# Attention with pooled keys, top-k rows and an MLP: high and low values side by side in one product, the scaling of the rows moved to ScalarE, one turned tile in the last batch

## The chip, the cores and the metric

One core of one Trainium2 chip. The time is device microseconds of one execution: 983.64 us before, the median of 3 runs (982.88 to 988.36). The names of the engines in the rows are PE (TensorE, with PEld for its weight loads), DVE (VectorE), ACT (ScalarE), POOL (GpSimd) and SP (SyncE, which issues the DMAs).

## The reference

```python
def _attn_ref(q, kv, w_sr):          # q: 4 x 12288 x 128, kv: 4 x 384 x 32 x 128
    kv_pool = kv.reshape(B, H // r, r, W // r, r, C).mean(axis=(2, 4))   # r = 4
    kv_flat = kv_pool.reshape(B, -1, C) @ w_sr                           # 768 keys of 128
    k = v = kv_flat
    s = scale * (q @ k.transpose(0, 2, 1))
    s = s - s.max(-1, keepdims=True)
    a = np.exp(s)
    a /= a.sum(-1, keepdims=True) + 1e-09
    return a @ v

def _moe_ref(x, w_gate, w1, w2, capacity):   # capacity = 128 rows per batch
    scores = np.einsum('bsd,d->bs', x, w_gate)
    out = x.copy()
    for b in range(B):
        top_idx = np.argpartition(-scores[b], capacity)[:capacity]
        xe = x[b, top_idx]
        ye = np.maximum(xe @ w1, 0.0) @ w2
        g = 1.0 / (1.0 + np.exp(-scores[b, top_idx]))
        out[b, top_idx] = x[b, top_idx] + g[:, None] * ye
    return out
```

The result is float32. Nearly all of the work is the attention: 49,152 queries against 768 keys of their batch.

## The kernel before, in words

**Tiling.** The four batches are cut into 192 blocks of 256 queries, 48 blocks per batch. A block has two halves (j = 0 and 1) of 128 queries, and the 768 keys make KT = 6 tiles of 128. The scores of a block, two halves of 768 columns, fill three PSUM banks; there are two such buffers (`s_buf`, s in the rows), used by turns. The remaining two banks are `o_two`, one for the output of each half. It exists once.

**Exactness by splitting.** Scores are made of three products (`S`): high query by low key (kl), low query (ql) by rounded key (kb), and high query by high key (kh). The exponentials are split into a float16 high part `ah` and a bfloat16 low part `al`, the values into a high and a low float16 part `vx[0]` and `vx[1]`. Each value tile has VC = 130 columns: 128 values, a column of ones (whose product is the sum of the weights), and the gate's score of the key. The low part has 0 in the column of ones.

**A block's way.** `S` writes the scores on PE. `s_max` takes the negated maximum of each half on DVE (m in the rows). `exp` makes the exponentials on ACT in three parts, part 2 (512 columns, the last bank) first, then part 1 and part 0 (am in the rows). The weights must then be turned so that keys lie on the partitions. Most tiles are turned by a DMA transpose (`turn`, rows at<-hl): ACT copies the high part (`to_high`), POOL or DVE subtracts to get the low part (`to_low`), and one transpose for each follows. The last `turned(n)` key tiles of a block are turned on PE instead (`turn_pe`, rows s<-cst,am): 1 in even blocks and 2 in odd blocks of batches 0 to 2, none in batch 3. They go from PSUM straight into `at` (rows at<-s). Where fewer than two are turned, part 1 (`own`, 256 columns) goes through its own copies (rows hl<-s). `AV` multiplies turned weights by values: per half, 6 x 2 products of `ah` by high and low values, then 6 of `al` by high values, all 130 columns wide, summed in one bank of `o_two`.

**The end of a block.** `sums` and `recip` make the reciprocal rz of the sums on DVE. `finish` multiplies the gate's column (rows sc<-o_two,rz) and the 128 columns of both halves (rows x<-o_two,rz) by rz, both on DVE. Four blocks share one tile x, which SP then stores.

**Order.** A helper (L54 in every row) chains the instructions of each engine in the order in which the program issues them, so each compute engine works in written order. Iteration i of the main loop writes s_max(i), AV of block i-4, the exponentials of block i, PE's turned tiles, scores of block i+1 in four parts, the end of block i-4, and the copies of block i. The turned tiles stand on PE behind the first of the four score parts. In front of every second block's exponentials ACT splits the queries of two blocks (`split_q`, rows qh<-q_raw). Three side tasks run in slots between: the next batch's keys (pooling on POOL, projection on PE, copies on ACT, rows kv_proj, kh, kb, vx), the top-k search of the batch before (rows junk, up, th, cnt), and its MLP. SP's order is not written out; the scheduler that builds the program places the DMAs.

Of the kernel before, what the change touches and what calls it, by code (L numbers as in the profile page):

```python
# [6 lines left out]
F32 = mybir.dt.float32  # L7
F32R = mybir.dt.float32r
F16 = mybir.dt.float16
# [4 lines left out]
AF = mybir.ActivationFunctionType  # L14
# [5 lines left out]
P = 128  # L20
# [48 lines left out]
def attention_topk_mlp(ctx, tc, a, outs, capacity):  # L69
# [34 lines left out]

    o_two = ps_o.tile([P, QT, 512], F32, name="o_two")
    o_all = o_two[:, :, 0:VC]
    banks = [o_two[:, j] for j in range(QT)]
    room = {"used": False}

# [33 lines left out]
    def new_keys(b):  # L143
        kvset[b] = {
            "kh": keys.tile([P, M], F32R, name="kh"),
            "kl": keys.tile([P, M], BF16, name="kl"),
            "kb": keys.tile([P, M], BF16, name="kb"),
            "raw": keys.tile([P, KT, 2, P], F32, name="kv_proj"),
            "vw": keys.tile([P, KT], F32, name="vw"),
            "mx": keys.tile([P, 4], F32, name="mx"),  # L150
            "vx": keys.tile([P, 2, KT, VC], F16, name="vx"),
            "sg": keys.tile([P, 4], F32, name="sg"),
        }

# [232 lines left out]
        st[n] = {"m": m}  # L387

    def turned(n):
        return 0 if blocks[n][0] == B - 1 else 1 + n % 2  # L390

    def own(n):
        return OWN if turned(n) < 2 else 0
# [59 lines left out]
    def turn(n, h):  # L453
        nc.sync.dma_start_transpose(out=st[n]["at"][:, h, 0:QT * KT - turned(n)], in_=st[n]["hl"][:, h, 0:main(n) + own(n)])

    def AV(n, j, dest=None):
        vx = kvset[blocks[n][0]]["vx"]
        assert kvset[blocks[n][0]].get("ready")
        ah, al = (st[n]["at"][:, h, j * KT:(j + 1) * KT].bitcast(t) for h, t in enumerate((F16, BF16)))
        if j == 0:  # L460
            st[n]["o"] = o_all if dest is None else dest
        o = st[n]["o"][:, j]
        tiles = list(range(KT))
        if j and own(n):
            tiles = tiles[2:KT - turned(n)] + tiles[0:2] + tiles[KT - turned(n):]
        mm = [(ah, h, kt) for kt in range(KT) for h in range(2)] + [(al, 0, kt) for kt in range(KT)]
        for i, (w, h, kt) in enumerate(mm):
            pe.matmul(o, w[:, kt], vx[:, h, tiles[kt]], start=(i == 0), stop=(i == len(mm) - 1))
# [11 lines left out]
    def finish(n):  # L480
        b, blk = blocks[n]
        o, rz = st[n]["o"], st[n]["rz"]
        if blk % GROUP == 0:
            xt_[b] = ob.tile([P, GROUP * QT, C], F32, name="x")
        x = xt_[b]
        if b not in scores:
            scores[b] = tk.tile([P, NCOL], F32, name="sc")
        if n < nb - 2:
            dve.tensor_tensor(out=scores[b][:, blk * QT:(blk + 1) * QT], in0=o[:, :, C + 1], in1=rz, op=ALU.mult)
        dve.tensor_tensor(out=x[:, (blk % GROUP) * QT:(blk % GROUP + 1) * QT], in0=o[:, :, 0:C], in1=rz.rearrange("p (j o) -> p j o", o=1).broadcast_to([P, QT, C]), op=ALU.mult)  # L490
        if blk % GROUP == GROUP - 1:
            ch, h = divmod(blk // GROUP, BPC // GROUP)
            nc.sync.dma_start(out=outs[b].rearrange("(h p j) d -> h p j d", p=P, j=JPC)[ch, :, h * GROUP * QT:(h + 1) * GROUP * QT], in_=x)
        del st[n]

    def topk(b):
# [167 lines left out]
    nc.sync.dma_start(out=w1, in_=a["w1"])  # L664
    nc.sync.dma_start(out=w2, in_=a["w2"].rearrange("(t f) d -> f t d", f=P))

    select, prep, vals, ended = [], [], [], []

    def start(tasks, gen):
        tasks.append([gen, next(gen)])  # L670
# [7 lines left out]
    def at_point(point):  # L678
        advance(vals, point)
        advance(prep, point)  # L680
        advance(select, point)
# [4 lines left out]
    for i in range(nb):  # L686
# [66 lines left out]
        else:  # L753
# [3 lines left out]
                dve.tensor_tensor(out=l, in0=x, in1=h, op=ALU.subtract)  # L757
            turn(i, 0)
            turn(i, 1)
        at_point("d")  # L760
        if old and blocks[m][1] == NBLK - 1:
            start(select, topk(blocks[m][0]))
# [120 lines left out]
```

## Time and profile before

| | |
|---|---|
| median of 3 runs | 983.64 us (982.88 to 988.36) |
| the profiled execution | 982.0 us, its span 980.2 us |
| granted TensorE clock, mean of the span | 0.973 |
| PE busy | 901.0 us (92%), 9995 products |
| DVE busy | 741.5 us (76%) |
| ACT busy | 749.0 us (76%) |
| POOL busy | 719.9 us (73%) |
| chain that ended last | PE 61%, DMA 13%, DVE 12%, ACT 6%, issue 5% |
| DMA | 216.02 MB, 384 transposes, 4.4 us from issue to landing in the median |

All rows are of the one profiled execution. The span is the time from its first to its last instruction. Busy is time in which an engine worked on at least one instruction; products overlap in PE's pipeline, so one product's duration is longer than the time until the next begins. Batches 0, 1 and 2 end near 250, 485 and 725 us, the last block's products near 936, and behind it stand the last batch's top-k and MLP.

### The profile page before, as it was taken

The page shows a single profiled execution, that of the slowest core. Times are in us where ns is not written, and L with a number is a line of the kernel's source. Part 1 is how long each engine was busy: PE and PEld are TensorE (multiplying, and loading weights), DVE is VectorE, ACT ScalarE, POOL GpSimd, SP SyncE. Part 2 cuts the span into 40 slices and gives each one's busy share as a digit, 9 for nine tenths or more (in the row PEclk, how much of TensorE's full clock was granted, in tenths as well). Part 3 has the DMA queues.
Part 4 walks back from the last instruction along what each step waited for, and adds up shares of the span by engine and source line. Part 5 has one row for each costly group of instructions (what it writes and reads, how often), then busy time and mean ns, then how long its engine had stood idle before and what let it go on. Part 6 is the DMA issues. An engine that isn't in the chain of part 4 may idle for free.

```text
span 980.2 us, 25939 instructions
## 1 busy us (share of the span) xinstructions
PE 901.0 (92%) x9995; PEld 719.2 (73%) x9995; DVE 741.5 (76%) x2000; ACT 749.0 (76%) x1241; POOL 719.9 (73%) x487
## 2 busy tenths in 40 slices
PE   4799899999999999999899999999899999999844
PEld 4577777777778778787677777787687777777743
DVE  5766677667788788788778877888868878778775
ACT  2588688888988787888788887888798878978600
POOL 2588788887788888888688886888678767767500
PEclk9999999999999999999999999999999999999976
DMA  9899999999999999999979999999899999999910
GB/s 357 215 236 223 233 231 240 256 230 244 226 227 231 241 233 243 243 233 233 219 169 232 240 234 230 225 216 201 191 190 227 235 240 236 235 244 221 220 28 6
DMA packets 568540, 216.02 MB, mean 220 GB/s; under 512 B 549216, under 2 KB 550368, under 8 KB 567648
## 3 DMA queue, kind: packets, MB, share of 16 engines
q1 hardware_dynamic: 568160, 213.84, 104.4%
q8 instruction: 78, 1.28, 0.5%
q0 software_dynamic: 256, 0.52, 0.2%
q14 instruction: 46, 0.38, 0.1%
HBM read 52.04 MB, written 25.43 MB: 79 GB/s over the span
## 4 chain that ended last, share of the span: by engine, by line
PE 61%; DMA 13%; DVE 12%; ACT 6%; issue 5%; POOL 2%; SPq 0%; POOLq 0%; DVEq 0%; ACTq 0%
PE s L54 34%; PE o_two L54 27%; DMA at<-hl 11%; DVE m L54 6%; ACT am L54 3%; DMA kv_raw<-in_kv 2%; ACT hl L54 1%; DVE junk L54 1%; POOL ql L54 1%; DVE sg L54 1%; ACT s L54 1%; DVE idx L54 1%; DVE hl L54 1%; POOL kv_sum L54 0%; DVE mg L54 0%
## 5 line engine op out<-in xcount | busy, mean ns | idle before, releaser
L54 POOL TENSOR_TENSOR hl<-am,hl 128x1280 bf16<-128x1280 f32 (+1 forms) x191 | 483.3, 2530 | 186.4 <-ACT hl L54 153.4
L54 PEld LDWEIGHTS <-at 128*128 128x128 f16 (+1 forms) x6912 | 401.4, 97 | 75.2 <-issue 48.9
L54 PE MATMUL o_two<-vx,at 128*128 128x130 f16 x6804 | 436.2, 220 | 19.1 <-DMA at<-hl 17.0
L54 DVE TENSOR_REDUCE m<-s 128x2 f32<-128x1536 f32 x192 | 337.2, 1757 | 114.0 <-PE s L54 113.5
L54 ACT ACTIVATE am<-s,m 128x512 f32<-128x512 f32 (+2 forms) x456 | 332.0, 744 | 105.0 <-DVE m L54 96.7
L54 PE MATMUL s<-kh,qh 128*128 128x512 f32 (+1 forms) x768 | 364.1, 476 | 0.0
L54 PE MATMUL s<-kl,qh 128*128 128x512 bf16 (+1 forms) x768 | 257.1, 335 | 3.0 <-DVE hl L54 1.7
L54 PE MATMUL s<-kb,ql 128*128 128x512 bf16 (+1 forms) x768 | 252.2, 328 | 1.1 <-POOL ql L54 0.9
L54 ACT CAST hl<-am 128x1152 f16<-128x1152 f32 (+1 forms) x192 | 236.1, 1230 | 2.3
L54 PEld LDWEIGHTS s<-kh,qh 128*128 128x128 f32 x768 | 147.3, 192 | 49.8 <-issue 1.4
L54 POOL TENSOR_TENSOR ql<-q_raw,qh 128x512 bf16<-128x512 f32 x96 | 122.7, 1278 | 6.2 <-ACT qh L54 6.2
L54 PEld LDWEIGHTS <-qh 128*128 128x128 bf16 x768 | 78.1, 102 | 32.7 <-issue 16.0
L54 PEld LDWEIGHTS <-ql 128*128 128x128 bf16 x768 | 76.2, 99 | 9.2 <-issue 3.6
L54 DVE TENSOR_TENSOR x<-o_two,rz 128x256 f32<-128x256 f32 x189 | 78.3, 414 | 0.0
L54 DVE TENSOR_TENSOR at<-s,at 128x128 bf16<-128x128 f32 (+1 forms) x144 | 51.2, 356 | 31.2 <-ACT at L54 29.2
L54 ACT CAST at<-s 128x128 f16<-128x128 f32 (+1 forms) x144 | 45.9, 319 | 35.0 <-PE s L54 34.7
L54 PE MATMUL s<-cst,am 128*128 128x128 f32 x216 | 53.6, 303 | 13.7 <-ACT am L54 13.1
L54 DVE TENSOR_SCALAR rz<-o_two,sg 128x2 f32<-128x2 f32 x189 | 40.9, 216 | 31.7 <-PE o_two L54 31.3
L54 PEld LDWEIGHTS s<-cst,am 128*128 128x128 f32 x216 | 26.2, 141 | 48.6 <-ACT am L54 45.2
L54 ACT CAST qh<-q_raw 128x512 fp32r<-128x512 f32 x96 | 59.2, 617 | 1.1 <-DMA q_raw<-in_q 1.1
L54 ACT ACTIVATE s<-s,m 128x256 f32<-128x256 f32 x120 | 53.8, 448 | 3.9
L54 POOL TENSOR_TENSOR kv_sum<-kv_raw 128x256 f32<-128x256 f32 x72 | 53.1, 737 | 0.0
(171 smaller groups left out, 622.9 us busy)
## 6 DMA issues: line engine op xcount, KB each, us to landing
out<-x SPq DMA_DIRECT2D x48, 512.0 KB, 3.7
q_raw<-in_q SPq DMA_DIRECT2D x46, 512.0 KB, 5.5
kv_raw<-in_kv SPq DMA_DIRECT2D x36, 512.0 KB, 5.1
kv_raw<-in_kv SPq DMA_DIRECT2D x6, 1024.0 KB, 7.3
at<-hl SPq DMA_TRANSPOSE x384, 4.4
w<-in_w SPq DMA_DIRECT2D x2, 512.0 KB, 9.1
q_raw<-in_q SPq DMA_DIRECT2D x1, 768.0 KB, 8.3
cst<-in_cst SPq DMA_DIRECT2D x1, 320.0 KB, 9.7
```

What stands on the lines that cost most here:

```text
L54: r = f(*args, **kwargs)
```

## The change

The tile vx keeps the high and the low half of each key tile side by side, and in the main loop one product of 260 columns multiplies `ah` by both; the output of a half then has 260 columns in its bank. The six products of `al` by the high half stay as they were and are added to the first 130 columns. `finish` no longer reads the finished sum from PSUM: DVE adds the two groups of 130 columns into a new SBUF tile t (a reduction over pairs that lie 130 columns apart), takes the gate's column from t, and ACT scales the 128 columns of each half by rz, one ACTIVATE per half. These two are issued at the end of the iteration, behind the copies of block i, and the store follows them. The last four blocks keep the old form. In batch 3 one key tile per block is turned on PE instead of none.

```diff
+    o_pair = o_two[:, :, 0:2 * VC].rearrange("p j (h c) -> p j c h", h=2)
...
-            "vx": keys.tile([P, 2, KT, VC], F16, name="vx"),
+            "vx": keys.tile([P, KT, 2, VC], F16, name="vx").rearrange("p t h c -> p h t c"),
...
     def turned(n):
-        return 0 if blocks[n][0] == B - 1 else 1 + n % 2
+        return 1 if blocks[n][0] == B - 1 else 1 + n % 2
...
+        if dest is None:
+            o = o_two[:, j, 0:2 * VC]
+            for kt in range(KT):
+                pe.matmul(o, ah[:, kt], vx[:, :, tiles[kt]].rearrange("p h c -> p (h c)"), start=(kt == 0), stop=False)
+            for kt in range(KT):
+                pe.matmul(o[:, 0:VC], al[:, kt], vx[:, 0, tiles[kt]], start=False, stop=(kt == KT - 1))
+            return
...
+        if not ended:
+            t = ob.tile([P, QT, VC], F32, name="t")
+            dve.tensor_reduce(out=t, in_=o_pair, axis=AX.X, op=ALU.add)
+            dve.scalar_tensor_tensor(out=gate, in0=t[:, :, C + 1], scalar=1.0, in1=rz, op0=ALU.mult, op1=ALU.mult)
+
+            def scaled():
+                for j in range(QT):
+                    act.activation(rows[:, j], t[:, j, 0:C], AF.Copy, scale=rz[:, j:j + 1])
+                store()
+
+            late.append(scaled)
+        else:
+            if n < nb - 2:
+                dve.tensor_tensor(out=gate, in0=o[:, :, C + 1], in1=rz, op=ALU.mult)
+            dve.tensor_tensor(out=rows, in0=o[:, :, 0:C], in1=rz.rearrange("p (j o) -> p j o", o=1).broadcast_to([P, QT, C]), op=ALU.mult)
+            store()
...
+        while late:
+            late.pop(0)()
         at_point("d")
```

How it moves the instructions is shown at three places. The first is ACT around the end of an odd block of batch 1 (s_111) and the start of the even one (s_110): hl is the copy of the high weights, qh the split of the queries, am and s the exponentials. Before:

```order
L54 ACTIVATE am<-s_111,m 128x768
L54 CAST hl<-am 128x1280
L54 CAST qh<-q_raw 128x512
L54 ACTIVATE am<-s_110,m 128x512
L54 ACTIVATE s_110<-s_110,m 128x256
```

And now:

```order
L54 ACTIVATE am<-s_111,m 128x768
L54 CAST hl<-am 128x1280
L54 ACTIVATE x<-t,rz 128x128 x2
L54 CAST qh<-q_raw 128x512
L54 ACTIVATE am<-s_110,m 128x512
L54 ACTIVATE s_110<-s_110,m 128x256
```

Two instructions now stand between hl and qh, and so ahead of the even block's first exponential; in even blocks they stand between hl and the odd block's first exponential.

The second place is DVE in a block of batch 3, from the reciprocal's input to the next maximum; up, th and junk belong to the top-k search. Before:

```order
L54 TENSOR_SCALAR junk,cnt<-key,th 128x96
L54 TENSOR_SCALAR rz<-o_two,sg 128x2
L54 RECIPROCAL rz<-rz 128x2
L54 TENSOR_TENSOR sc<-o_two,rz 128x2
L54 TENSOR_TENSOR x<-o_two,rz 128x256
L54 TENSOR_REDUCE m<-s_111 128x2
```

And now:

```order
L54 TENSOR_SCALAR junk,cnt<-key,th 128x96
L54 TENSOR_SCALAR rz<-o_two,sg 128x2
L54 RECIPROCAL rz<-rz 128x2
L54 TENSOR_REDUCE t<-o_two 128x260
L54 SCALAR_TENSOR_TENSOR sc<-t,rz 128x2
L54 TENSOR_TENSOR at<-s_110,at 128x128
L54 TENSOR_REDUCE m<-s_111 128x2
```

The reduction t takes the place of x as the last reader of o_two, sc now reads t, and the low part of the turned tile stands ahead of the next maximum.

The third place is SP in batch 3: transposes (at), stores (out) and loads of queries (q_raw). Before:

```order
L493 DMA out<-x 128x1024
L454 DMA_TRANSPOSE at<-hl 128x12x128 x2
L139 DMA q_raw<-in_q 128x1024 x2
L454 DMA_TRANSPOSE at<-hl 128x12x128 x6
L493 DMA out<-x 128x1024
```

And now:

```order
L501 DMA out<-x 128x1024
L455 DMA_TRANSPOSE at<-hl 128x11x128
L140 DMA q_raw<-in_q 128x1024
L455 DMA_TRANSPOSE at<-hl 128x11x128 x2
L140 DMA q_raw<-in_q 128x1024
L455 DMA_TRANSPOSE at<-hl 128x11x128 x5
L501 DMA out<-x 128x1024
```

The store goes behind the first transpose of a block instead of ahead of it, and the two loads of queries no longer follow each other. Over the whole program two loads of queries stand back to back 18 times before and 4 times now, with two transposes between them 4 times before and 18 times now. Two loads of raw keys stand back to back 5 times before and 10 times now.

## Rows read from the trace of the kernel before

**Rows 1.** Page, part 1: engine, busy us (share of the span), instructions.
```profile
PE 901.0 (92%) x9995; PEld 719.2 (73%) x9995; DVE 741.5 (76%) x2000; ACT 749.0 (76%) x1241; POOL 719.9 (73%) x487
```

**Rows 2.** Waits, 60 to 725 us: who waited for whom: us, times, longest.
```profile
PEld s L54 <- ACT am L54: 39.8, 96, 3.3
...
PE o_two L54 <- DMA at<-hl: 13.1, 15, 2.5
```

**Rows 3.** Timeline of ACT, batch 1: start us, duration us, instruction [idle before].
```profile
308.20 1.26 ACT L54 CAST hl<-am 128x1280 f16<-128x1280 f32 x1
309.36 0.61 ACT L54 CAST qh<-q_raw 128x512 fp32r<-128x512 f32 x1
310.21 0.69 ACT L54 ACTIVATE am<-s,m 128x512 f32<-128x512 f32 x1 [0.24 <-DVE up L54]
...
312.53 1.17 ACT L54 CAST hl<-am 128x1152 f16<-128x1152 f32 x1
```

**Rows 4.** Timeline of PE in the same even block.
```profile
308.17 1.20 PE L54 MATMUL o_two<-vx,at 128*128 128x130 f16 x18
...
309.24 1.19 PE L54 MATMUL o_two<-vx,at 128*128 128x130 f16 x18
...
310.95 0.33 PE L54 MATMUL s<-cst,am 128*128 128x128 f32 x1
311.12 0.27 PE L54 MATMUL s<-kl,qh 128*128 128x256 bf16 x1
311.23 0.27 PE L54 MATMUL s<-kb,ql 128*128 128x256 bf16 x1
```

**Rows 5.** Timeline of DVE, the odd block's end, the even block and the next maximum.
```profile
307.05 0.16 DVE L54 TENSOR_TENSOR sc<-o_two,rz 128x2 f32<-128x2 f32 x1
307.12 0.42 DVE L54 TENSOR_TENSOR x<-o_two,rz 128x256 f32<-128x256 f32 x1
...
308.36 1.76 DVE L54 TENSOR_REDUCE m<-s 128x2 f32<-128x1536 f32 x1 [0.49 <-PE s L54]
...
312.69 1.76 DVE L54 TENSOR_REDUCE m<-s 128x2 f32<-128x1536 f32 x1 [0.78 <-PE s L54]
```

**Rows 6.** Timeline of ACT, an even block near the start of batch 1.
```profile
255.61 0.41 ACT L54 CAST vx<-kv_proj 128x256 f16<-128x256 f32 x1
255.92 0.61 ACT L54 CAST qh<-q_raw 128x512 fp32r<-128x512 f32 x1
256.44 0.68 ACT L54 ACTIVATE am<-s,m 128x512 f32<-128x512 f32 x1
```

**Rows 7.** Timeline of DVE, the maxima of that even block and the next.
```profile
254.08 1.76 DVE L54 TENSOR_REDUCE m<-s 128x2 f32<-128x1536 f32 x1 [0.55 <-PE s L54]
...
258.92 1.76 DVE L54 TENSOR_REDUCE m<-s 128x2 f32<-128x1536 f32 x1 [0.79 <-PE s L54]
```

**Rows 8.** Groups by line and shape: count | busy us, mean ns | idle before.
```profile
L54 ACT ACTIVATE kv_proj<-kv_proj,sg 128x256 f32<-128x256 f32 x9 | 4.6, 512 | 0.0
...
L54 DVE TENSOR_REDUCE mg<-s 128x2 f32<-128x256 f32 x4 | 1.6, 412 | 0.0
```

**Rows 9.** Timeline of SP in batch 3, DMA issues.
```profile
772.83 1.00 SPq L139 DMA_DIRECT2D q_raw<-in_q  x2
773.93 10.22 SPq L454 DMA_TRANSPOSE at<-hl  x4
```

**Rows 10.** Timeline of PE behind those loads.
```profile
783.69 0.52 PE L54 MATMUL o_two<-vx,at 128*128 128x130 f16 x6 [1.90 <-DMA at<-hl]
...
784.08 2.09 PE L54 MATMUL o_two<-vx,at 128*128 128x130 f16 x18
```

**Rows 11.** Timeline of DVE, two maxima in batch 3.
```profile
764.51 1.76 DVE L54 TENSOR_REDUCE m<-s 128x2 f32<-128x1536 f32 x1 [0.54 <-PE s L54]
...
768.67 1.76 DVE L54 TENSOR_REDUCE m<-s 128x2 f32<-128x1536 f32 x1 [0.54 <-PE s L54]
```

More of the change, by code (lines that the diff above doesn't have):

```diff
@@ L487, in finish, with store @@
             scores[b] = tk.tile([P, NCOL], F32, name="sc")
[L488 to L493, printed above, removed]
+        rows = x[:, (blk % GROUP) * QT:(blk % GROUP + 1) * QT]
+        def store():
+            if blk % GROUP == GROUP - 1:
+                ch, h = divmod(blk // GROUP, BPC // GROUP)
+                nc.sync.dma_start(out=outs[b].rearrange("(h p j) d -> h p j d", p=P, j=JPC)[ch, :, h * GROUP * QT:(h + 1) * GROUP * QT], in_=x)
+        gate = scores[b][:, blk * QT:(blk + 1) * QT]
+        if not ended:
[12 more added lines that the diff above has]
+            store()
         del st[n]
@@ L665, in attention_topk_mlp @@
     nc.sync.dma_start(out=w2, in_=a["w2"].rearrange("(t f) d -> f t d", f=P))
-    select, prep, vals, ended = [], [], [], []
+    select, prep, vals, ended, late = [], [], [], [], []
     def start(tasks, gen):
```

## The prediction

> **What bounds the kernel now.** I read the page's busy table first, then the waits of batches 0 to 2, then one odd and one even block of the timeline on each engine. The table gives no clear winner: DVE and ACT both have 76% [rows 1]. The waits say more. Between 60 and 725 us, the weights of a turned tile waited 96 times for ACT's am [rows 2]. This stretch holds 140 blocks, so in most of them PE stands still at that place.
>
> The timeline shows the ring behind it. In the even block DVE's maximum m begins at 308.36 and takes 1.76 [rows 5]; ACT's exponential of bank 2 begins at 310.21, 0.09 later, and ends at 310.90 [rows 3]; the turned tile's product begins at 310.95 [rows 4]; three score groups follow, and the next m begins at 312.69 [rows 5]. That is 4.33 us from m to m. (The odd block, with two turned tiles, takes 4.44.) The products o_two are not on this ring. PE does them while DVE and ACT work, and then waits for the exponential: ring and PE are nearly equal, and the ring is the longer one. So an exponential that begins late lengthens the block one for one. The trace has the proof: at 256.44 it begins 0.51 late, since ACT had two more instructions in front of it [rows 6], and that block lasts 4.84 (254.08 to 258.92) instead of 4.33 [rows 7].
>
> In batch 3 nothing is turned, there is no such ring, and m follows m after 4.16 [rows 11]: there PE is the bound. On top of both come waits for transposes, 13.1 us in 15 places in batches 0 to 2 [rows 2].
>
> **The change, part by part.**
>
> *The product of 260 columns.* Per block 36 products of 130 columns become 12 of 260 and 12 of 130; the columns stay the same. Eighteen of 130 start within 1.07 us, with one short product of the search (0.03) among them, 58 ns each [rows 4]. A product of 256 columns is followed after 0.11 [rows 4], so 260 cost between 0.108 (columns alone) and 0.12; two of 130 cost 0.114 to 0.117. The twelve pairs of a block give between 0.07 us lost and 0.11 won; I take 0.045 won, by the 0.11 row. In batches 0 to 2 it is worth 0: PE then waits that much longer for the exponential.
>
> *DVE.* Removed are sc and x, 307.05 to 307.54, 0.49 us. Added is a sum over 520 PSUM values and a small product. The nearest reductions are mg with 256 values at 412 ns [rows 8] and m with 1536 at 1.76 [rows 5]: 1.05 ns per value and 0.14 besides, so 0.69, between 0.55 (without the 0.14) and 1.24 (if the two halves, 130 apart, went at half pace). With a step of 0.03 and sc's 0.16 that is 0.88: 0.39 more. DVE stands idle 0.49 before an even m and 0.78 before an odd one [rows 5], which covers it. o_two comes free 0.20 later; the next product begins 0.63 after x's end [rows 4, 5], so that is covered too. Not covered are blocks in which DVE goes from one thing to the next without idle time before m: 18 in batches 0 to 2, of which some 11 have no room behind m either. 11 x 0.39 = **+4.3**.
>
> *ACT.* Two scalings of 128 columns per block are new, SBUF to SBUF with a scale from memory. They stand behind the copy hl and ahead of the next qh. A cast of 256 columns in SBUF takes 0.41 but holds the engine only 0.31 (255.61 to 255.92, then qh begins) [rows 6]; 128 columns less take 0.09 to 0.11 off (hl 1.26 against 1.17 [rows 3]), so one of 128 holds it 0.20 to 0.22. The same 256 columns with a scale from memory take 0.512 [rows 8], 0.10 more. That makes 0.31 each and 0.62 a pair, between 0.41 (no price for the scale) and 0.81 (no overlap).
> By the Trainium skill, ScalarE: Activation LUTs, section What ACT_TABLE_LOAD costs, an ACTIVATE takes 186 ns and 0.833 per element, 93 more for a pointer operand, and neighbours overlap by 93: an estimate of 0.59 for the pair, with which the sum below would be about 1.5 us lower; the trace's 0.10 agrees roughly with its 93.
>
> Where does it land? In an odd block hl begins at 308.20, qh at 309.36, and qh holds ACT 0.52 (255.92 to 256.44), so ACT is free at 309.88 and the exponential is due at 310.21 [rows 3, 6]. Only 0.33 is free: 0.62 makes it **0.29 late**. In an even block hl begins at 312.53 and ACT is free 1.05 to 1.17 later; the next exponential is due at 312.69 + 1.76 + 0.09 = 314.54 [rows 3, 5], and 0.62 fits. So the price is 0.29 in each even block that is on the ring. Of 68 even blocks there, 16 have PE late by itself (transfers, projections) and 12 have ACT already late, as in rows 6; of the other 40, 7 are among the DVE cases. 33 x 0.29 = **+9.6**. The 12 pay the full 0.62, three of them less by room behind them: **+6.4**. Seven with a copy of projected keys pay 0.13: **+0.9**.
>
> *Transfers.* SP's program changes too. The store now waits for ACT and goes behind the high transpose, and the two half-megabyte loads of queries, back to back 18 times before and 4 times now, have two transposes between them. That matters: after the pair at 772.83 four transposes take 10.22 us [rows 9], and PE waits 1.90 and then runs eighteen products in 2.09 instead of 1.19 [rows 4, 10]. Waits and slow products together cost some 17 us in batches 0 to 2 (13.1 of waiting [rows 2] and two slow stretches of nearly 2), and 8.3 in batch 3 (rows 10 show one of two places with 1.90 of waiting and nearly as much of slow products, 3.8 together; a third is small). Key loads still come in pairs, so I take 70% of the 17, **-12**, between 0 and all.
>
> *The turned tile of batch 3.* Transposes there shrink from 12 to 11 tiles, so I take all the stalls as gone: **-8.3**. But the tile puts batch 3 on the ring: 4.33 (the even block above, also with one tile) instead of 4.16, and ACT now needs 312.53 - 310.21 + 1.05 = 3.37, and 0.62, and 0.52 in every second block: 4.51, late by 0.18. A pair costs 2 x 0.17 + 0.18 = 0.53; 17 undisturbed pairs, **+9.0**; 12 blocks at both ends, where ACT or DVE already runs late, about 0.4 each, **+5.0**. DVE there gains 0.39 and the tile's 0.29 and loses 0.54 + 0.17 of idle time: just covered.
>
> Sum: 4.3 + 9.6 + 6.4 + 0.9 - 12 - 8.3 + 9.0 + 5.0 = +14.9. The profiled execution took 982.0 (span 980.2), which gives 996.9. The median of the runs is 1.6 above it; I say **998**. With the scaling at 0.41 and 0.81, and transfers from no relief to full, this case runs from 985 to 1014.
>
> **The rivals.**
> *Transfers outweigh the ring (faster).* A single mechanism decides: how long ACT holds a scaled half. If the pair costs 0.41 or less, an even block loses 0.08 only: 2.6 + 4 + 4.3, batch 3 7 to 9; and if all 25 us of stalls go, about -6: 977. It turns the sign where the pair is under 0.4 and no load pair holds the transposes up any more. For it: the stalls follow load pairs [rows 9, 10]. Against it: the scale's 0.10 us. 0.12.
> *PE sets the pace (faster).* Then the wide product wins 0.045 x 183 = 8 us, the tile in batch 3 costs 0.17 x 46 = 8, the stalls give back 20: 963. The Trainium skill, Perfetto Trace Analysis, section Matmuls, says that larger matmuls are more efficient; two of 58 ns against one of 0.11 us agree, but by little. Against it: 96 waits for am. 0.05.
> *Gains and losses cancel.* Pair near 0.45, relief near 20: 984 to 988, no change. 0.16.
> *The reduction runs at half pace (slower still).* DVE's addition becomes 0.94: 0.45 late in even, 0.15 in odd blocks, 0.5 in batch 3: near 1050. No row shows values 130 apart. 0.06.
>
> **How the numbers follow.** The main case has 0.61; 998 is its time. Half a per cent, 4.9 us, is about what a measurement of this kernel tells from no change. Faster 0.17, same 0.16 and a little of the main case's lower end, slower the rest: 0.17, 0.18, 0.65. The range leaves out PE's case, the half-pace case and the tails of the main one: 974 to 1016.
>
> **What would show it.** Right: in even blocks ACT's am waits no longer for m, m to m is near 4.62 there and 4.44 in odd ones, batch 3 alternates near 4.33 and 4.51, and PE's waits for am grow. Waits of o_two for transposes fall below 6 us. The scaling pair holds ACT 0.6. Wrong: even blocks stay at 4.33 (then the pair is cheap), or o_two waits for t (then the reduction is slow), or o_two still waits over 10 us for transposes.

## The result, and the profile after

The changed kernel takes **996.42 us** (median of 4 runs, 993.37 to 999.17) against 983.26 us for the kernel before in the same comparison (4 runs, 981.95 to 988.36). The ratio is 1.0131, 95% interval 1.0086 to 1.0176: slower, by more than the 0.5% that a measurement of this kernel can tell. The profiled execution took 993.37 us, its span 991.6.

From the page of the changed kernel, in order: busy time per engine, the chain that ended last (its first line), and the groups that the change made or touched (busy us, mean ns of one | idle time before).

```profile
PE 906.4 (91%) x7787; PEld 677.9 (68%) x7787; DVE 845.4 (85%) x2048; ACT 850.2 (86%) x1665; POOL 709.1 (72%) x487
...
PE 34%; DVE 28%; ACT 19%; issue 12%; DMA 5%; POOL 1%; DVEq 0%; SPq 0%; POOLq 0%; ACTq 0%
...
L54 PE MATMUL o_two<-vx,at 128*128 128x260 f16 (+1 forms) x4548 | 423.6, 246 | 2.7 <-DMA at<-hl 2.0
...
L54 ACT ACTIVATE x<-t,rz 128x128 f32<-128x128 f32 x376 | 131.9, 405 | 0.0
...
L54 DVE TENSOR_REDUCE t<-o_two 128x260 f32<-128x520 f32 x188 | 127.5, 678 | 0.0
...
L54 DVE SCALAR_TENSOR_TENSOR sc<-t,rz 128x2 f32<-128x2 f32 x188 | 97.1, 516 | 6.5
```

DVE and ACT went from 76% to 85 and 86% [rows 1], and the chain that ended last now runs through them (28% and 19%, where it had 12% and 6%). The reduction t takes 678 ns, as forecast. The small product sc takes 516, where 160 had been counted: that is the surprise.

The waits between 60 and 725 us, the stretch of [rows 2] (us in total, times, longest):

```profile
PEld s L54 <- ACT am L54: 73.2, 125, 1.6
DVE m L54 <- PE s L54: 46.9, 91, 1.1
PE s L54 <- ACT am L54: 25.5, 54, 1.2
ACT am L54 <- DVE m L54: 24.7, 59, 1.5
...
PE o_two L54 <- DMA at<-hl: 2.0, 3, 1.4
```

The weight loads of PE's turned tiles wait longer for ACT's exponentials (73.2 us, 39.8 before), and o_two hardly waits for transposes (2.0 us, 13.1 before) [rows 2]. Both had been forecast. The mechanism on ACT stands in its timeline, with DVE's maxima beside it, around an even block of batch 1 (start, duration, instruction, in brackets the idle time before it):

```profile
311.31 1.26 ACT L54 CAST hl<-am 128x1280 f16<-128x1280 f32 x1
312.47 0.69 ACT L54 ACTIVATE x<-t,rz 128x128 f32<-128x128 f32 x2
313.07 0.60 ACT L54 CAST qh<-q_raw 128x512 fp32r<-128x512 f32 x1
313.58 0.68 ACT L54 ACTIVATE am<-s,m 128x512 f32<-128x512 f32 x1
```

```profile
307.03 1.76 DVE L54 TENSOR_REDUCE m<-s 128x2 f32<-128x1536 f32 x1 [0.56 <-PE s L54]
...
311.48 1.75 DVE L54 TENSOR_REDUCE m<-s 128x2 f32<-128x1536 f32 x1
...
316.04 1.76 DVE L54 TENSOR_REDUCE m<-s 128x2 f32<-128x1536 f32 x1 [0.51 <-PE s L54]
```

The pair of scalings holds ACT from 312.47 to 313.07, 0.60. The maximum of the even block ends at 313.23, and its exponential begins at 313.58, 0.35 later instead of the 0.09 of [rows 3, 5]: 0.26 late, with no idle time of ACT before it. From 311.48 to 316.04 the block lasts 4.56; it was 4.33 before. The odd block ahead of it (307.03 to 311.48, 4.45) is as it was.

In batch 3 something else goes on. DVE's and GpSimd's timelines there, two blocks:

```profile
775.99 0.68 DVE L54 TENSOR_REDUCE t<-o_two 128x260 f32<-128x520 f32 x1
776.70 1.06 DVE L54 SCALAR_TENSOR_TENSOR sc<-t,rz 128x2 f32<-128x2 f32 x1
777.69 0.28 DVE L54 TENSOR_TENSOR at<-s,at 128x128 bf16<-128x128 f32 x1
777.89 1.74 DVE L54 TENSOR_REDUCE m<-s 128x2 f32<-128x1536 f32 x1
...
781.59 0.16 DVE L54 SCALAR_TENSOR_TENSOR sc<-t,rz 128x2 f32<-128x2 f32 x1
...
782.20 1.76 DVE L54 TENSOR_REDUCE m<-s 128x2 f32<-128x1536 f32 x1 [0.24 <-PE s L54]
```

```profile
774.13 2.38 POOL L54 TENSOR_TENSOR hl<-am,hl 128x1152 bf16<-128x1152 f32 x1 [2.35 <-PE s L54]
776.47 1.28 POOL L54 TENSOR_TENSOR ql<-q_raw,qh 128x512 bf16<-128x512 f32 x1
778.61 2.37 POOL L54 TENSOR_TENSOR hl<-am,hl 128x1152 bf16<-128x1152 f32 x1 [0.86 <-DVE at L54]
```

The sc at 776.70 lasts until 777.76; GpSimd's ql, at work since 776.47, ends at 777.75. The next m follows with no idle time before it: here DVE sets the pace. One block later GpSimd is done (its hl ends at 780.98) when sc begins at 781.59, sc takes 0.16, and DVE has 0.24 of idle time. Of all 188 such sc, 157 begin while GpSimd works on one of its two-operand instructions. 139 of these take longer than 163 ns, and all of the 139 end 14 to 33 ns behind the end of a GpSimd instruction: 135 of the one in which they began, four of the one after it. The other 49 sc take 160 to 163 ns. The old sc, with one operand in PSUM, began inside such an instruction 176 times in the profile of before and never took more than 163 ns. The Trainium skill has the rule (SBUF — State Buffer, section SBUF: two separate sides): a DVE instruction with two SBUF inputs and a GpSimd instruction that reads SBUF need the same port pair, and whoever comes second stands still until the first is done. The rows agree.

Where the time went, by stages, from the start of m in block 8, in block 144 and in the last block, as the timelines have them:

| | batches 0 to 2 | batch 3 | the rest behind it |
|---|---|---|---|
| before | 644.1 | 210.3 | 59.3 |
| changed | 648.5 | 219.4 | 57.3 |
| difference | +4.4 | +9.1 | -2.0 |

The rest lay between 57.3 and 61.0 in all the profiles of this study; its -2.0 lies within that spread. The stages, here and below, are those of one profiled execution per kernel: the two profiled ones differ by 11.4 us, the medians by 13.2.

Part of what a wait for a transpose costs stands in no list of waits. After the wait that ends at 783.69 in the kernel before [rows 10], TensorE's granted clock fell from 2.4 to 1.2 GHz (start and end, length, busy us of PE, PEld, DVE, ACT and POOL with instructions, granted clock, then DMA):

```profile
780.00:784.00 4.00, 2.10 (x25) 1.50 (x24) 2.64 (x5) 3.83 (x6) 2.47 (x2) 1.00 1.18 186
784.10:787.40 3.30, 3.30 (x25) 2.51 (x23) 1.58 (x8) 2.37 (x4) 2.99 (x3) 0.50 1.28 227
787.60:791.00 3.40, 3.40 (x47) 2.92 (x46) 2.02 (x3) 0.17 (x1) 1.64 (x1) 1.00 1.15 319
```

The eighteen slow products of [rows 10] (2.09 us instead of 1.19) lie in that stretch. The kernel before spends 10.2 us of batches 0 to 2 and 6.8 us of batch 3 at 1.2 GHz, in five stretches of 3.4 us. Four of them begin within 1.6 us behind a wait for a transpose of 1.9 to 2.5 us, the fifth at the end of a wait of 2.8 us for ACT's exponentials; behind another such wait, near 704, the clock stayed up. The profiled execution of the changed kernel has no such stretch in either stage.

### The profile page after: what moved, and what is told of

Its sections match the earlier page's. It is cut to its first block, busy times and chain, and to the rows that moved or that the text cites. A ratio compares the mean times of both kernels' runs of the same rounds, so it can differ in the third digit from the quotient of the medians.

```text
span 991.6 us, 21995 instructions
## 1 busy us (share of the span) xinstructions
PE 906.4 (91%) x7787; PEld 677.9 (68%) x7787; DVE 845.4 (85%) x2048; ACT 850.2 (86%) x1665; POOL 709.1 (72%) x487
## 4 chain that ended last, share of the span: by engine, by line
PE 34%; DVE 28%; ACT 19%; issue 12%; DMA 5%; POOL 1%; DVEq 0%; SPq 0%; POOLq 0%; ACTq 0%
PE s L54 23%; DVE m L54 11%; PE o_two L54 11%; ACT am L54 10%; ACT hl L54 4%; DMA at<-hl 3%; DVE sc L54 3%; DVE t L54 3%; DVE junk L54 2%; ACT x L54 2%; DVE hl L54 2%; DMA kv_raw<-in_kv 2%; DVE rz L54 1%; DVE at L54 1%; ACT qh L54 1%
## 5 line engine op out<-in xcount | busy, mean ns | idle before, releaser
L54 POOL TENSOR_TENSOR hl<-am,hl 128x1152 bf16<-128x1152 f32 (+1 forms) x191 | 471.6, 2469 | 210.8 <-ACT hl L54 122.7
L54 PE MATMUL o_two<-vx,at 128*128 128x260 f16 (+1 forms) x4548 | 423.6, 246 | 2.7 <-DMA at<-hl 2.0
L54 PEld LDWEIGHTS <-at 128*128 128x128 f16 (+1 forms) x4656 | 358.0, 97 | 86.8 <-issue 50.3
L54 ACT CAST hl<-am 128x1152 f16<-128x1152 f32 x192 | 231.4, 1205 | 2.3
L54 ACT ACTIVATE x<-t,rz 128x128 f32<-128x128 f32 x376 | 131.9, 405 | 0.0
L54 DVE TENSOR_REDUCE t<-o_two 128x260 f32<-128x520 f32 x188 | 127.5, 678 | 0.0
L54 PE MATMUL s<-cst,am 128*128 128x128 f32 x264 | 69.9, 309 | 38.6 <-ACT am L54 35.2
L54 DVE SCALAR_TENSOR_TENSOR sc<-t,rz 128x2 f32<-128x2 f32 x188 | 97.1, 516 | 6.5
L54 ACT CAST at<-s 128x128 f16<-128x128 f32 x192 | 58.6, 305 | 15.8 <-PE s L54 15.6
L54 DVE TENSOR_TENSOR at<-s,at 128x128 bf16<-128x128 f32 x192 | 63.8, 332 | 9.2 <-ACT at L54 8.7
```

Source lines behind the costliest of these rows:

```text
L54: r = f(*args, **kwargs)
```

## The experiments

All ran beside the kernel before; each ratio is to it. "Waits" are the waits of o_two for transposes between 60 and 725 us.

| run | us | ratio, 95% interval | batches 0 to 2 | batch 3 | waits |
|---|---|---|---|---|---|
| sc from PSUM (1) | 986.23 | 1.0024 (0.9994 to 1.0054) | 649.9 | 213.4 | 8.5 |
| no tile in batch 3 (2) | 988.98 | 1.0062 (1.0037 to 1.0086) | 649.8 | 208.2 | 3.1 |
| before, loads apart (3) | 986.62 | 1.0043 (1.001 to 1.0075) | 649.8 | 209.8 | 16.2 |
| changed, loads apart (4) | 994.58 | 1.0115 (1.0082 to 1.0148) | 649.0 | 219.5 | 1.8 |
| scalings spread (5) | 985.29 | 1.0039 (1.0023 to 1.0054) | 641.4 | 218.9 | 1.6 |
| before + tile (6) | 980.4 | 0.9985 (0.9961 to 1.0009) | 646.4 | 209.8 | 14.6 |
| before, loads by ACT (7) | 990.12 | 1.0077 (1.0052 to 1.0101) | | | |
| before, no loads (8) | 957.64 | 0.9759 (0.9734 to 0.9784) | 626.4 | 202.6 | none |
| before + wide product (9) | 976.02 | 0.9916 (0.9884 to 0.9948) | 646.0 | 204.7 | 15.7 |
| changed, loads in pairs (10) | 1046.35 | 1.0644 (1.0604 to 1.0684) | 695.6 | 222.1 | none |
| both mends (11) | 971.31 | 0.9874 (0.9845 to 0.9903) | 634.1 | 210.7 | 3.3 |
| both mends, no tile (12) | 969.45 | 0.9865 (0.9834 to 0.9895) | 633.8 | 210.9 | 2.6 |

**1. The small product from PSUM.**

```diff
-            dve.scalar_tensor_tensor(out=gate, in0=t[:, :, C + 1], scalar=1.0, in1=rz, op0=ALU.mult, op1=ALU.mult)
+            dve.tensor_tensor(out=gate, in0=o_two[:, :, C + 1], in1=rz, op=ALU.mult)
```

> The changed kernel, with the small product sc taken from PSUM (column 129 of o_two's first half) and not from t in SBUF; it leaves out the low half's part of the gate's column, so that part of the gate's scores is missing, and nothing else changes. Theory: sc, with both operands in SBUF, stands still until the tensor_tensor that GpSimd is running ends; that makes sc 516 ns on average where 160 was counted, and in batch 3 DVE has no room left and sets the pace. Then sc falls to about 160 ns here, the pair of blocks in batch 3 from 9.21 us to about 8.85, batch 3 is 7 to 9 us shorter, batches 0 to 2 some 2 to 4 shorter: 984 to 990 us. Rival 1: ACT's late exponential holds batch 3 (the ring alone): sc falls, DVE's idle time before m grows by the same, the time stays at 994 to 998. Rival 2: sc is slow because of the strided read of column 129 of t, or because it queues behind something else on DVE: then the durations follow t or not at all, and sc does not bunch at the end of GpSimd's operations in the changed kernel.

986.23 us. The rows of sc in its profile (x count, ns min/median/max) and three of DVE's maxima in batch 3:

```profile
L54 DVE TENSOR_TENSOR sc<-o_two,rz x189: 146/150/160, 47.3 to 937.5; 128x2 f32<-128x2 f32 x189
```

```profile
782.79 1.76 DVE L54 TENSOR_REDUCE m<-s 128x2 f32<-128x1536 f32 x1 [0.38 <-PE s L54]
...
787.28 1.76 DVE L54 TENSOR_REDUCE m<-s 128x2 f32<-128x1536 f32 x1 [0.54 <-PE s L54]
...
791.61 1.76 DVE L54 TENSOR_REDUCE m<-s 128x2 f32<-128x1536 f32 x1 [0.38 <-PE s L54]
```

sc never exceeds 160 ns, DVE has idle time again before nearly every m, and a pair of blocks takes 4.49 + 4.33 = 8.82, where the changed kernel has 9.21 (4.31 + 4.90). Batch 3 is 6.0 shorter (expected 7 to 9). For batch 3 the theory holds; rivals 1 and 2 fall. Batches 0 to 2 do not show the 2 to 4 that were expected, but the stalls hide what they gained: waits for transposes came back to 8.5 us, and 10.2 us were spent at 1.2 GHz. As an estimate, the waits and half of the time at 1.2 GHz, where products take nearly twice as long, make 13.6 us here and 2.0 in the changed kernel; with these taken off both, batches 0 to 2 are some 10 us shorter than there. The profiled execution is also one of the run's longest (990.07; all twelve from 979.5 to 990.93), and the changed kernel's is the shortest of its four.

**2. The changed kernel without the tile in batch 3.**

```diff
-        return 1 if blocks[n][0] == B - 1 else 1 + n % 2
+        return 0 if blocks[n][0] == B - 1 else 1 + n % 2
```

> The changed kernel without the turned tile in batch 3 (its turned() gives 0 there again, as before the change). Theory: with no tile there is no ring in batch 3, ACT's 0.25 late no longer counts, and DVE loses the tile's 0.29 us; the pace is PE's 4.16 per block or DVE's own sum, 4.2 to 4.3: a pair of 8.4 to 8.6 where the changed kernel has 9.21, 23 pairs, 14 to 19 us less; since the query loads stay two transposes apart, no waits of more than 3 us in sum for transposes come back: 978 to 984 us. Rival 1: it is the tile (11 instead of 12 tiles to transpose) that removed the transfer stalls of batch 3, not the order of the loads: then 6 to 9 us of waits of o_two for transposes come back there, 986 to 992. Rival 2: DVE alone sets batch 3's pace whatever PE does: a pair of 9.21 less twice 0.29 is 8.63, and DVE shows no idle time before m in any block.

988.98 us, above all that the theory allowed; batch 3 took 208.2, 11.2 less than with the tile, not 14 to 19. Its pair of blocks takes 4.52 + 4.01 = 8.53, close to rival 2's 8.63. Three maxima, and the sc ahead of the second, on DVE; then GpSimd beside it:

```profile
776.06 1.74 DVE L54 TENSOR_REDUCE m<-s 128x2 f32<-128x1536 f32 x1
...
779.76 0.90 DVE L54 SCALAR_TENSOR_TENSOR sc<-t,rz 128x2 f32<-128x2 f32 x1
780.58 1.74 DVE L54 TENSOR_REDUCE m<-s 128x2 f32<-128x1536 f32 x1
...
784.59 1.74 DVE L54 TENSOR_REDUCE m<-s 128x2 f32<-128x1536 f32 x1
```

```profile
778.01 2.63 POOL L54 TENSOR_TENSOR hl<-am,hl 128x1280 bf16<-128x1280 f32 x1 [0.67 <-DVE m L54]
```

sc stands from 779.76 to 780.66, until GpSimd's hl is done at 780.64. In 33 of the 36 blocks of batch 3's main stretch m has no idle time before it: DVE sets the pace of batch 3 even with its work on the tile gone. The waits for transposes that rival 1 wanted did not come back at that pace (0.9 us in batch 3); that the time lies in its 986 to 992 is chance.

**3 and 4. The query loads apart, in either kernel.** Loads and transposes are chained in written order on SP's program, and a load is written two blocks later:

```diff
+    pe, dve, act, pool, sp = (InOrder(tc, e) for e in (nc.tensor, nc.vector, nc.scalar, nc.gpsimd, nc.sync))
...
-        nc.sync.dma_start(out=qraw[b, ch][:, lo:hi], in_=a["q"][:, b, ch, lo:hi])
+        sp.dma_start(out=qraw[b, ch][:, lo:hi], in_=a["q"][:, b, ch, lo:hi])
...
-        nc.sync.dma_start_transpose(out=st[n]["at"][:, h, 0:QT * KT - turned(n)], in_=st[n]["hl"][:, h, 0:main(n) + own(n)])
+        sp.dma_start_transpose(out=st[n]["at"][:, h, 0:QT * KT - turned(n)], in_=st[n]["hl"][:, h, 0:main(n) + own(n)])
...
-        if blk % GROUP == 0 and i + BPC < nb:
-            nb_, nblk = blocks[i + BPC]
+        if blk % GROUP == 2 and i - 2 + BPC < nb:
+            nb_, nblk = blocks[i - 2 + BPC]
```

> The kernel before, with nothing changed but SyncE's program: the two half-megabyte query loads of a chunk, which the order before put back to back 18 times, are each placed four blocks apart, with eight transposes between them (loads and transposes keep the order in which they are written, and a load is written two blocks later). The programs of PE, DVE, ACT and GpSimd are the same row by row. Theory: the pairs of loads are what the transposes wait behind; the waits of o_two for transposes (13 us in batches 0 to 2) and the slow products beside them fall to under 3 us, batches 0 to 2 are 10 to 17 us shorter and batch 3 about 8: 958 to 966 us against 983. Rival 1: half of the stalls come from key loads and stores, whose places hardly change: 970 to 975. Rival 2: the stalls are hidden, since the ring waits anyway at those blocks: 980 to 984.

> The changed kernel with the same placing of the query loads (four blocks apart). Theory: the changed kernel has already been freed of nearly all its transfer stalls by having two transposes between two loads, with 5 us of waits for transposes left; so only 1 to 5 us go: 991 to 996. Rival: the stalls that remained are only those which PE shows as waits, and the slow products beside transfers cost as much again: 984 to 990.

The kernel before with its loads apart takes 986.62 us: no gain at all, where 958 to 966 had been expected. Its waits between 60 and 725 us:

```profile
PE o_two L54 <- DMA at<-hl: 16.2, 14, 2.8
```

They are as long as with the pairs (13.1). So it is not the pairing of the loads that makes the stalls, and all three expectations for this run were wrong in their mechanism; rival 2's 980 to 984 is nearest in time. In the changed kernel the same edit gave 994.58 us, inside what was expected (991 to 996) and among the changed kernel's own times (993.37 to 999.17); so the written order, which the edit also fixes for SP, costs nothing that shows there.

**5. The scalings spread.** On top of run 4, each half is an entry of its own:

```diff
-            late.append(scaled)
+            late.extend((scaled, j) for j in range(QT))
...
-        while late:
-            late.pop(0)()
+        for _ in range(1 if i % 2 else 3):
+            if late:
+                f, j = late.pop(0)
+                f(j)
```

> The changed kernel with the query loads four blocks apart (as in the run before this one) and ACT's scalings spread by hand: one half at the end of an odd block, three at the end of an even one, so that what stands between hl and the next exponential fits both times. Theory of the ring: the even blocks' exponential is no longer 0.25 late, their period falls from 4.58 to about 4.34, some 33 blocks, 7 to 9 us less in batches 0 to 2, and batch 3, where DVE sets the pace, hardly moves: 984 to 988 against 994.6. Theory of the full transfer path: the transposes cannot follow at that pace; the period of undisturbed even blocks falls to 4.34 but waits of o_two for transposes come back (2 us now, 8 to 14 then), batches 0 to 2 lose at most 4 us: 989 to 995. Rival: the lateness is not the scaling pair's; the even blocks stay at 4.57.

985.29 us; batches 0 to 2 are 7.6 shorter than in run 4 (7 to 9 expected by the ring), batch 3 hardly moves (0.5). On ACT:

```profile
311.50 1.00 ACT L54 ACTIVATE x<-t,rz 128x128 f32<-128x128 f32 x3
312.47 1.05 ACT L54 ACTIVATE am<-s,m 128x512 f32<-128x512 f32 x2
...
316.06 0.40 ACT L54 ACTIVATE x<-t,rz 128x128 f32<-128x128 f32 x1
316.36 0.60 ACT L54 CAST qh<-q_raw 128x512 fp32r<-128x512 f32 x1
316.91 0.69 ACT L54 ACTIVATE am<-s,m 128x512 f32<-128x512 f32 x1
```

Three halves fit ahead of one exponential, one half and qh ahead of the other; the undisturbed even block is back at 4.33. ACT's lateness is shown as a price of the change, and the waits for transposes did not come back with the faster pace (1.6 us): the theory of the full transfer path fails here.

**6. The tile alone, in the kernel before.** The edit is the reverse of run 2's, in the kernel before.

> The kernel before with one turned tile in batch 3 and nothing else of the change. Theory: the tile puts batch 3 on the ring, 4.33 per block instead of 4.15 (0.17 x 44 blocks = 7.7 us more), and takes one twelfth of the transposes away, so that the 8 us of waits there vanish although the query loads still come in pairs: batch 3 stays within 2 us of 210, 980 to 986 in all. Rival 1: the pairs of loads are what makes the stalls: half or more of the 8 us stay, 986 to 992. Rival 2: the ring does not bind in batch 3: 4.15 stays and the stalls go, 972 to 977.

980.4 us. Three maxima of batch 3:

```profile
781.95 1.76 DVE L54 TENSOR_REDUCE m<-s 128x2 f32<-128x1536 f32 x1 [0.51 <-PE s L54]
786.27 1.76 DVE L54 TENSOR_REDUCE m<-s 128x2 f32<-128x1536 f32 x1 [0.51 <-PE s L54]
790.60 1.76 DVE L54 TENSOR_REDUCE m<-s 128x2 f32<-128x1536 f32 x1 [0.51 <-PE s L54]
```

4.33 per block, as the ring of an even block says; and no wait of o_two for a transpose is left in batch 3, though the loads still come in pairs. The ring costs 7.2 there (209.8 against run 8's 202.6), the stalls that go were worth 7.7, and batch 3 ends 0.5 shorter. The theory holds, both rivals fall.

**7. The loads issued by ACT** (kernel before): the load of the main loop goes to `act`, behind `turn(i, 0)` of every second even block.

```diff
-        if blk % GROUP == 0 and i + BPC < nb:
-            nb_, nblk = blocks[i + BPC]
-            load_q(nb_, nblk // BPC, nblk % BPC * BLK, (nblk % BPC + GROUP) * BLK)
...
+            if blk % GROUP == 2 and i - 2 + BPC < nb:
+                nb_, nblk = blocks[i - 2 + BPC]
+                load_q(nb_, nblk // BPC, nblk % BPC * BLK, (nblk % BPC + GROUP) * BLK, act)
             to_low(i, 0, pool)
```

> The kernel before with the query loads of the main loop issued by ACT instead of SyncE, at the end of every second even block, where ACT has about a microsecond to spare. Nothing else moves. SyncE was 90% busy issuing in the kernel before (transposes 1.9 us each, 1.3 where nothing is ahead of them). Theory A, SyncE's one queue is full: freed of 46 loads, the transposes follow at once, waits of o_two for transposes fall from 21 us to under 6: 962 to 972. Theory B, the sixteen DMA engines themselves are full, whoever issues: the waits stay, 978 to 986. Theory C, the issue holds ACT long enough to make exponentials late: periods of the blocks behind a load grow, 985 to 995.

990.12 us (977.96 to 1002.84). The 962 to 972 of theory A, that SP's queue alone is full, did not come; the time lies in C's range. The time alone does not show whether A's gain was there and ACT's issuing ate it. Nothing points to it: the mean granted clock of the executions was 0.960 to 0.973, lower than the 0.969 to 0.981 of the kernel before beside them, where run 8, without stalls, had 0.975 to 0.981. The profile is of the longest execution, 1002.84 us, and is not used here; B and C stay open.

**8. No loads** (kernel before): the main loop's loads are left out.

```diff
-            load_q(nb_, nblk // BPC, nblk % BPC * BLK, (nblk % BPC + GROUP) * BLK)
+            qraw[nb_, nblk // BPC] = qraw[0, 0]
```

> The kernel before without the query loads of the main loop: every block works on the first chunk's queries, so the output is that of repeated queries. The programs of PE, DVE, ACT and GpSimd stay as they are. This is what the loads cost at most. Theory of the full transfer path: with 24 MB less to move, the waits for transposes vanish (under 3 us) and so do the slow products, 960 to 968. Rival 1: the transposes alone fill the path: waits of 8 us or more stay, 972 to 980. Rival 2: the stalls are hidden by the ring: 978 to 984.

957.64 us. In batches 0 to 2 and batch 3 no wait of o_two for a transpose is left. Nor is there any stretch at 1.2 GHz. The two stages are 17.7 and 7.7 shorter than before: that is what transfer stalls cost in the kernel before, and what the prediction had taken from waits and slow products (17 and 8.3). An estimate from the rows of before agrees: the waits, 13.1 and 3.9, and half of the time at 1.2 GHz, 5.1 and 3.4, make 18.2 and 7.3. The run also gives the pace without transfers, 626.4 and 202.6, against which the other costs can be read.

**9. The wide product alone** (kernel before, the diff's lines of vx and AV; DVE's sc and x as before).

> The kernel before with the 260-column products alone: values' halves side by side, twelve products of 260 and twelve of 130 columns. DVE takes the first 130 columns as before; the high weights' product with the low values is computed but not added to the output. Theory: PE gains about 0.09 us per block (with the tile taken out of batch 3 the changed kernel's blocks there came every 4.06 instead of 4.15), which shows only where PE sets the pace: nothing in batches 0 to 2 (4.33 and 4.44 stay), 44 x 0.09 = 4 us in batch 3 as far as transposes follow: 977 to 982. Rival 1: the transposes can't follow and PE's gain turns into waits for them: 981 to 985. Rival 2: PE also sets the pace in batches 0 to 2: 4.33 becomes 4.24 or so, 965 to 972.

976.02 us, 0.84% less than before. In batch 3 the undisturbed blocks come every 4.11 instead of 4.15:

```profile
757.11 1.76 DVE L54 TENSOR_REDUCE m<-s 128x2 f32<-128x1536 f32 x1 [0.50 <-PE s L54]
761.22 1.76 DVE L54 TENSOR_REDUCE m<-s 128x2 f32<-128x1536 f32 x1 [0.49 <-PE s L54]
```

0.04 per block, half of what was expected for this run, and just the 0.045 of the prediction; 44 x 0.04 = 1.8 us. The rest of batch 3's 5.6 us less comes with fewer stalls there (2.6 us of waits for transposes for 3.9, and no time at 1.2 GHz for 6.8); why they are fewer no run shows. In batches 0 to 2 it gains nothing (646.0 against 644.1; undisturbed blocks stay at 4.33 and 4.44), since the ring sets the pace: rival 2 falls.

**10. The changed kernel with the loads in pairs.** Both loads of a chunk are written behind `turn(i, 0)` of each fourth block of eight, with SP's program chained as in run 4.

```diff
-        if blk % GROUP == 0 and i + BPC < nb:
-            nb_, nblk = blocks[i + BPC]
-            load_q(nb_, nblk // BPC, nblk % BPC * BLK, (nblk % BPC + GROUP) * BLK)
...
+            if blk % BPC == 4 and i - 4 + BPC < nb:
+                nb_, nblk = blocks[i - 4 + BPC]
+                for h in range(2):
+                    load_q(nb_, nblk // BPC, h * GROUP * BLK, (h + 1) * GROUP * BLK)
             to_low(i, 0, pool)
```

> The changed kernel with the query loads put back in pairs, all 23 back to back, two transposes behind a store (the pattern of the kernel before); the programs of PE, DVE and ACT stay the same. Theory P, the pace: the changed kernel has few stalls because its own blocks are slower, above all where key tiles are copied; then the pairs do little, waits of o_two for transposes stay under 5 us in batches 0 to 2 and batch 3, 994 to 999. Theory O, the order (the one the prediction gave): the pairs bring the stalls back, 8 to 14 us of waits and as many of slow products beside them, less what the slower blocks cover: 1000 to 1010.

1046.35 us, far outside both. The waits say why:

```profile
ACT qh L54 <- DMA q_raw<-in_q: 36.9, 15, 5.2
```

I had put the pairs so late that ACT waits for the queries themselves. There are no waits of o_two for transposes, but at that pace this tells nothing about the order of loads: the run settles neither theory.

**11 and 12. Both mends, with and without the tile.** Run 5, and sc on GpSimd, behind the low half's subtraction; run 12 has `turned` 0 in batch 3 besides.

```diff
-            dve.scalar_tensor_tensor(out=gate, in0=t[:, :, C + 1], scalar=1.0, in1=rz, op0=ALU.mult, op1=ALU.mult)
...
+            def scaled(j):
+                if j == 0:
+                    pool.tensor_tensor(out=gate, in0=t[:, :, C + 1], in1=rz, op=ALU.mult)
```

> The changed kernel with two mends: the small product sc goes to GpSimd, behind its own subtraction, and ACT's scalings are spread, one half at the end of an odd block and three at the end of an even one (query loads four blocks apart). Theory: with the scalings spread alone the time was 985.3; sc off DVE gives back the 6 us of batch 3, and with ACT and DVE both in time batch 3 is on the ring alone, 4.33 per block, 4 us more: 972 to 977, less than either kernel. Rival 1: GpSimd's two-operand product now stands still behind DVE, or DVE's additions behind it, and delays the low halves: transposes late, 980 to 988. Rival 2: at this pace the transfers are full again and 6 to 10 us of waits come back: 980 to 986.

> The same two mends without the turned tile in batch 3. Theory: batch 3 has no ring and DVE and ACT have room, so PE sets the pace at 4.06 to 4.15: 44 blocks, 8 to 11 us less than with the tile, less 2 to 4 us of waits for transposes: 966 to 972. Rival 1, full transfer path: at 4.06 twelve tiles of transposes per half cannot follow, 8 us or more of waits: 974 to 980. Rival 2: DVE still sets the pace there, 4.25 or more per block: 974 to 978, with few waits.

971.31 and 969.45 us: both faster than either kernel, by 1.3% against before. On GpSimd sc is short:

```profile
L54 POOL TENSOR_TENSOR sc<-t,rz x188: 182/193/214, 52.1 to 914.6; 128x2 f32<-128x2 f32 x188
```

Batches 0 to 2 take 634.1 (641.4 in run 5): sc had cost 7.3 us there as well, and the new freedom was not eaten by transposes. Batch 3 is on the ring at 4.33 with the tile. Without it the undisturbed blocks come every 4.11, as the theory said (15 blocks of batch 3):

```profile
733.27 1.76 DVE L54 TENSOR_REDUCE m<-s 128x2 f32<-128x1536 f32 x1 [0.43 <-PE s L54]
737.38 1.76 DVE L54 TENSOR_REDUCE m<-s 128x2 f32<-128x1536 f32 x1 [0.43 <-PE s L54]
```

But transposes are waited for again, 6.4 us in batch 3, the clock is at 1.2 GHz for 3.4 us around the end of the longest of these waits, and eleven blocks take 4.23 to 4.29, nine of them in a row, in which PE works almost without a gap; why, no run shows. So the 8 to 11 us expected from taking the tile out are eaten (210.9 against 210.7), mostly by the stalls that rival 1 named; the time fell into the theory's range because batches 0 to 2 and the mends put it there.

## Why the prediction was right, point by point

The sign, the time (998 against 996.42) and the main mechanism were right. That the time came so near is partly luck, as two errors of opposite sign stood in the sum. Forecast by stages: batches 0 to 2 +9.2, batch 3 +5.7, measured +4.4 and +9.1.

*The product of 260 columns:* right. 0.045 per block forecast, 0.04 measured where PE sets the pace (run 9), nothing on the ring.

*ACT, the pair 0.62 and 0.29 late:* right; 0.60 and 0.26 in the timeline. The even blocks' price of 9.6 measured as 7.6 (run 5 against run 4; some blocks stay late there).

*DVE, +0.39 per block:* the reduction was right (0.69 forecast, 678 ns). The step that failed is "sc's 0.16": it took the old sc's duration, whose operand lay in PSUM, for one with both operands in SBUF. It measured 516 ns in the mean, by GpSimd's hold (run 1). So DVE loses 0.73 per block in the mean instead of 0.39. "Just covered" in batch 3 fails with it: the pair of blocks was forecast at 8.84, came at 9.21, and is 8.82 once sc is mended. The hold of sc costs 6.0 us in batch 3 (run 1) and 7.3 in batches 0 to 2 (run 11 against run 5), where the forecast had nothing and 4.3 for all of DVE.

*Ring costs together in batches 0 to 2:* 4.3 + 9.6 + 6.4 + 0.9 = 21.2 forecast; the changed kernel takes 22.1 more than the pace without loads (648.5 against 626.4), waits of 2.0 included. The total held, though sc's part in it was larger than thought and the others smaller.

*Transfers:* the size of the stalls was right (17 and 8.3 forecast, 17.7 and 7.7 measured in run 8); their slow products were read off rightly, but not as what they are, products at 1.2 GHz. The relief was taken too small: -12, where waits of 2.0 and no time at 1.2 GHz are left of the 17.7. The reason given, that the loads "have two transposes between them", is refuted: loads put apart by themselves remove nothing (run 3). In batch 3 the tile does it, by leaving eleven tiles to transpose (run 6), at the price of the ring. That half of the forecast, -8.3 with ring costs of about the same size, was right. In batches 0 to 2 the cause stays open. The runs that keep the store and the end of a block as before waited 13.1 to 16.2 us there (before, 3, 6, 9), those with the changed end 1.6 to 8.5 (1, 2, 4, 5, 11, 12); the pace of undisturbed blocks is not it, as 11 runs them at the pace of before. The store's new place behind the high transpose was not tried by itself.

*The rivals:* "Transfers outweigh the ring" asked for a pair of 0.41, and it is 0.60. "PE sets the pace" falls with 4.56 in even blocks and with run 9. "The reduction runs at half pace" falls at 678 ns. "Gains and losses cancel" asked for 0.45. Of the signs named for the forecast all came true (even blocks 4.56 for 4.62, odd ones 4.45, o_two's waits 2.0) but one: batch 3 alternates between 4.31 and 4.90, not 4.33 and 4.51.

## What to carry to other kernels

Before a small operation is moved off PSUM, look at what its new operands share with other engines: a product of two columns became the pace of a whole stage because both its inputs then lay in SBUF beside a busy GpSimd. New work for an engine on a ring is best cut into pieces of the size of its gaps: the same 1.2 us per two blocks cost 7.6 us less as one piece and three than as two and two. And a forecast from waits can have the size of a stall right and its cause wrong; only taking the suspected cause away shows it. A stall's price is more than its wait: look at the granted clock behind it.

## What the runs showed of the hardware

A DVE product of 128 x 2 with both operands in SBUF took from 160 ns to 2.63 us: 160 to 163 ns 49 times, and 139 times until 14 to 33 ns behind the end of GpSimd's running or next instruction (188 in the changed kernel; longest 2632 ns). The profile books the whole stand as DVE's busy time, so that the wait shows in no list of waits. With one operand in PSUM the same product took 146 to 160 ns (run 1), and on GpSimd itself 182 to 214 (run 11).

A transpose of ten to twelve tiles holds SP for some 1.5 us in the median; the second one behind a load of queries held it 2.9 in the mean (run 3, 31 of them in batches 0 to 2), and 4.2 behind a pair of loads (before, the 4 in batch 3). SP was thus busy issuing for 90% of batches 0 to 2 in the kernel before, and a backlog lasts: in run 3 SP issues with no gap over 0.13 us from 406 to 440 us, and PE's longest stall of that stretch, 2.8 us, begins at 428.6. The granted clock is 0.50 from 430.6 to 437.5 there.
